# V of the second head group of batch 0 loaded ahead of all weights, into an output-weight buffer

## The chip, the cores and the metric

The kernel runs on 1 core of one Trainium2 chip. The metric is the device time of one execution in microseconds (us), less is better. Three executions of the kernel before took 917.45, 918.29 and 919.88 us; the median is 918.29 us.

## What is computed

An attention of Nystrom's kind feeds two gated feed-forward layers. B, H, S, D = 4, 8, 576, 64; 32 landmarks; 2304 tokens, model width 512, hidden width 1536.

```python
q_lm = q.reshape(B, H, m, S // m, D).mean(axis=3)      # m = 32
k_lm = k.reshape(B, H, m, S // m, D).mean(axis=3)
A  = sm(q, k_lm); Bm = sm(q_lm, k_lm); C = sm(q_lm, k) # softmax of the scaled product
Z = Bm^T / (norm1(Bm) * norminf(Bm) + 1e-06)           # norms of each matrix
for _ in range(6):
    Z = 2 * Z - Z @ Bm @ Z
attn = A @ Z @ C @ v
x  = silu(x @ w_gate) * (x @ w_val) @ w_out            # first layer, x from attn
x  = sigmoid(x @ w_gate2) * (x @ w_val2) @ w_out2      # second layer
```

All inputs and outputs are float32. V enters only in `C @ v`.

## The kernel before, in words

**Attention.** The eight heads of a batch are two groups of four, so there are eight pairs (b, g). For each pair a generator `front(b, g)` (F00, F01, F10, ... in the order string `first`, L575) does: K, then Q, summed over the 18 rows of a landmark on DVE (`lm`, L121), transposed on PE (`lt`, L125; `tp`, L135) and copied out by ACT; landmark scores (`cs`, L156), their exponentials on ACT (`e`, L162) and their transposes (`et`, L185, copied to `eT`, L186); then C @ V: 48 matmuls `cv` (L191) that read the tile `vin`, scaled on DVE into `bc` (L193); last the scores `as` (L204) with their maximum, difference and exponential (L207 to L210). `back(b)` (B0, B1, ...) takes the `bs` and `bc` of both groups of a batch: a chain of small DVE instructions makes the scale `rr` (L250 to L258), then come seven products `nw` (L267) on PE, each followed by one DVE instruction on `rw` (L273, L278 five times, L284), and a transpose to `ut` (L287). The products for group 1 read group 1's `bc`. While `back` iterates, it also steps `a_steps` (L213 to L228), the normalised and transposed A.

**First layer.** For chunk c of 256 hidden columns and batch b: `uw` (U00: `ut` times the input weights, L416), `gv1` (G00: gate and value matmuls into PSUM tiles `pg` and `pv`, Silu on ACT, product on DVE, split into a high and a low part) and `o1` (O00: `po`, added up in `acc`). The second layer, from about 250 us on, is not touched.

**Weights.** They arrive as pieces of 512 KB in three rotating `raw` buffers (L329). A piece of the input weights is four DMAs in layer 0 (L338), one of the output weights is one (L346). `convert` (L303) unpacks a piece with two ACT instructions (L314, L317) and two DVE instructions (L319, L323). For the output weights ACT and DVE then split the result (L350, L351) into the tile `wo` of tag "wo" (L368), of which there are two buffers of 8 KB a partition, one for each of two chunks in turn. Counted from 0, pieces 0 to 3 of chunk 0 are input weights, converted beside F00 (the word `I0`), and pieces 4 and 5 are its output weights; two pieces beyond the one in work are asked for ahead (`load_to`, L357).

**Loads of Q, K and V.** All are 576 KB DMAs on SP's queue, as are the weights, in one order. At the start K, Q, V of (0,0) and K, Q of (0,1) are issued (L294 to L296); there are four buffers for Q and K and one for V. Later ones are issued inside `front` by `load_next` (L85): K and Q two pairs ahead, as soon as their buffer is read; V one pair ahead, right after the `cv` matmuls that last read the single `vin` buffer (L194).

**The order of the work.** Python emits the instructions in the order of `first`, with weight conversions as filler between the words that begin with U, G or O. A scheduler at build time then gives each engine its final order, from the emitted order as a priority and from its own estimate of when operands are ready; each engine, and SP's queue, runs its list strictly in order. So an instruction can stand behind others that the code names later: in the trace the 54 last `as` matmuls of F01 stand ahead of its `cv`, though the code names `cv` first.

Of the kernel before, what the change touches and what calls it, by code (L numbers as in the profile page):

```python
# [5 lines left out]
F32 = mybir.dt.float32  # L6
# [8 lines left out]
def nystrom_moe_kernel(tc, q, k, v, wg1, wv1, wo1, wg2, wv2, wo2, out):  # L15
    nc = tc.nc
    B, H, S, D = q.shape
    M = 32
    P = 128
    L = S // M  # L20
    R = 6
    TP = S // R
    HS = S // 2
    DM = H * D
# [7 lines left out]
    def pool(name, side=None, **kw):  # L32
        return tc.alloc_tile_pool(name=name, bufs=1, side=side, reuse_waits="tile", **kw)

    cst = pool("cst")
    per = pool("per")
    att = pool("att")
# [28 lines left out]
    inq = {}  # L66

    def load_attn(b, which, g):
        if which == "v":
            t = att.tile([TP, 4, R, D], F32, tag="vin", name=f"vin{b}_{g}", bufs=1)  # L70
            nc.sync.dma_start(t, v[b, 4 * g:4 * g + 4].rearrange("h (p r) d -> p h r d", r=R))
        else:
            t = att.tile([P, L, D], F32, tag="in", name=f"{which}in{b}_{g}", bufs=4)
            src = {"q": q, "k": k}[which]
            nc.sync.dma_start(t, src[b, 4 * g:4 * g + 4].rearrange("h (t u) d -> (h t) u d", u=L))
        inq[which, b, g] = t
# [3 lines left out]
    AORDER = [(b, g) for b in range(B) for g in range(2)]  # L80
# [2 lines left out]
        return x.rearrange("p a b -> p (a b)")  # L83

    def load_next(b, g, which):  # L85
        i = AORDER.index((b, g)) + (1 if which == "v" else 2)
        if i < len(AORDER):
            load_attn(AORDER[i][0], which, AORDER[i][1])

    def step(fill, n=1):  # L90
# [20 lines left out]
    def front(b, g):  # L111
# [6 lines left out]
        def lm_steps(which):  # L118
            src = inq[which, b, g]
            lm = sm("lm", [P, 2, D])  # L120
            nc.vector.tensor_reduce(lm[:, 0], src.rearrange("p u d -> p d u"), axis=AX.X, op=ALU.add)  # L121
            nc.scalar.copy(lm[:, 1], lm[:, 0])
            yield
            ps = pst(b, [P, P], "lt", g)
            nc.tensor.transpose(ps, flat(lm), ident)  # L125
            bdt = sm("bd" + which, [P, 2, P], 1)
            for w in range(2):
                nc.scalar.activation(bdt[:, w], ps, AF.Copy, scale=pmask[:, w:w + 1])
            yield
            t = sm("kq", [P, NU, P])  # L130
            for i in range(3):
                ps = pst(b, [P, 3, P], "tp", g)
                for j in range(3):
                    u = 3 * i + j
                    nc.tensor.transpose(ps[:, j], flat(src[:, 2 * u:2 * u + 2]), ident)  # L135
                nc.scalar.copy(t[:, 3 * i:3 * i + 3], ps)
                yield
            load_next(b, g, which)
            return bdt, t
# [49 lines left out]
        for r in range(R):  # L189
            for h in range(4):  # L190
                mm(ps[32 * h:32 * h + 32, :], eT[:, r, 32 * h:32 * h + 32],  # L191
                   inq["v", b, g][:, h, r, :], start=(r == 0), stop=(r == R - 1))
        nc.vector.tensor_scalar(BC[:, g, M:M + D], ps, rc, None, op0=ALU.mult)  # L193
        load_next(b, g, "v")  # L194
        yield

# [95 lines left out]
            yield  # L292

    for g in range(2):  # L294
        for x in "kqv" if g == 0 else "kq":
            load_attn(0, x, g)  # L296


# [359 lines left out]
```

## Time and profile before

| | |
|---|---|
| runs | 917.45, 918.29, 919.88 us, median 918.29 |
| profiled execution, its own time | 917.74 us |
| span of its trace, first to last instruction | 915.9 us |
| PE busy / DVE busy / ACT busy | 877.8 / 542.2 / 391.7 us |
| granted TensorE clock, mean over the span | 0.987 of full speed |
| DMA moved | 57.66 MB |

The profiled execution lies 0.55 us under the median of the runs, and its trace leaves 1.84 us of its time outside the span. Times of rows are microseconds from the span's start unless they are marked ns. PE is TensorE, DVE VectorE, ACT ScalarE; SPq is SyncE's queue, which issues DMAs. A line such as L193 is a line of the kernel's code; matmuls issued through the helper `mm` all have line L62 and are told apart by their tiles. An instruction "waits" for what ended the idle time of its engine before it.

### The profile page before, as it was taken

How to read it: one execution, taken by the hardware profiler on the slowest of the kernel's cores; microseconds unless marked ns; L12 is line 12 of the kernel's file. 1: busy time of each engine (PE TensorE's matmuls, PEld its weight loads, DVE VectorE, ACT ScalarE, POOL GpSimd, SP SyncE). 2: the span in 40 equal slices, each digit the busy share in tenths (PEclk: the TensorE clock that was granted, in tenths of full speed). 3: DMA queues.
4: the chain of work that ended last, by engine and by line, in shares of the span. 5: the costliest groups of instructions: out<-in, count | busy, mean ns of one | idle time of the engine just before them, and what ended most of it. 6: DMA issues, size and time to landing. Idle time of an engine off the chain costs nothing.

```text
span 915.9 us, 16047 instructions
## 1 busy us (share of the span) xinstructions
PE 877.8 (96%) x6588; PEld 741.9 (81%) x6588; DVE 542.2 (59%) x1093; ACT 391.7 (43%) x853; POOL 0.7 (0%) x6
## 2 busy tenths in 40 slices
PE   5499899999999999999999999999999999999997
PEld 4356877778898998998998888888888888888886
DVE  6988857746968678769961154346238236323343
ACT  5568568545725446428652263134116114111111
POOL 0000000000000000000000000000000000000000
PEclk9599999999999999999999999999999999999999
DMA  7666211003513113203110022003004000000132
GB/s 230 222 209 182 70 53 49 7 1 93 155 31 93 47 47 116 69 1 95 46 44 4 0 71 68 1 28 110 0 1 138 1 1 24 1 0 1 47 93 69
DMA packets 27081, 57.66 MB, mean 63 GB/s; under 512 B 4224, under 2 KB 7296, under 8 KB 27008
## 3 DMA queue, kind: packets, MB, share of 16 engines
q1 hardware_dynamic: 25280, 54.28, 19.6%
q10 hardware_dynamic: 1728, 2.36, 1.1%
q8 instruction: 51, 0.84, 0.4%
q14 instruction: 22, 0.18, 0.1%
HBM read 51.90 MB, written 4.72 MB: 62 GB/s over the span
## 4 chain that ended last, share of the span: by engine, by line
PE 88%; DVE 5%; ACT 4%; DMA 1%; issue 1%; SPq 0%; ACTq 0%
PE po L62 33%; PE pg L62 24%; PE pv L62 23%; PE pu L62 3%; PE tp L135 2%; PE nw L62 1%; DMA qin<-in_q_dram 1%; DVE lm L121 1%; PE cs L62 1%; ACT e L162 1%; PE as L62 1%; DVE hl L351 0%; ACT L162 0%; PE et L185 0%; DVE h L441 0%
## 5 line engine op out<-in xcount | busy, mean ns | idle before, releaser
L62 PE MATMUL po<-hh,wo 128*128 128x288 f32 x768 | 162.1, 302 | 1.1 <-DVE uw L351 0.7
L512 DVE TENSOR_TENSOR hf<-hf,pv 128x512 f32<-128x512 f32 (+1 forms) x60 | 38.0, 634 | 193.0 <-PE pv L62 193.0
L62 PE MATMUL po<-wo,h 128*128 128x512 f32 x648 | 152.2, 390 | 0.0
L62 PEld LDWEIGHTS po<-wo,h 128*128 128x128 f32 x648 | 121.1, 188 | 25.4 <-ACT h L350 0.3
L62 PEld LDWEIGHTS po<-hh,wo 128*128 128x128 f32 x768 | 123.0, 188 | 21.1 <-issue 14.4
L62 PE MATMUL pg<-AH,w 128*128 128x512 f32 (+1 forms) x480 | 136.1, 368 | 0.0
L62 PE MATMUL pv<-AH,w 128*128 128x512 f32 (+1 forms) x480 | 136.0, 368 | 0.0
L62 PE MATMUL po<-hl,wo 128*128 128x288 f32 x384 | 114.8, 299 | 0.3 <-DVE hl L351 0.3
L511 ACT ACTIVATE hf<-pg 128x512 f32<-128x512 f32 (+1 forms) x60 | 33.2, 554 | 165.4 <-PE pg L62 158.3
L62 PE MATMUL pg<-AH,uw 128*128 128x288 f32 x576 | 98.7, 298 | 2.3 <-ACT uw L350 1.8
L62 PEld LDWEIGHTS pg<-AH,w 128*128 128x128 f32 x480 | 87.3, 188 | 15.4
L62 PEld LDWEIGHTS pv<-AH,w 128*128 128x128 f32 x480 | 87.1, 189 | 15.0
L62 PE MATMUL pv<-AH,uw 128*128 128x288 f32 x576 | 96.7, 296 | 1.2 <-ACT sg L439 1.2
L62 PEld LDWEIGHTS pg<-AH,uw 128*128 128x128 f32 x576 | 83.1, 188 | 8.4 <-ACT uw L350 4.9
L350 ACT CAST h<-hf 128x512 fp32r<-128x512 f32 (+1 forms) x60 | 34.6, 576 | 123.2 <-DVE hf L512 123.2
L533 DVE TENSOR_TENSOR oacc<-po,oacc 128x512 f32<-128x512 f32 x90 | 61.9, 691 | 41.1 <-PE po L62 39.9
L62 PEld LDWEIGHTS pv<-AH,uw 128*128 128x128 f32 x576 | 82.9, 188 | 3.2 <-ACT sg L439 2.2
L62 PE MATMUL pg<-x1l,w 128*128 128x512 f32 x192 | 74.7, 389 | 0.0
L62 PE MATMUL pv<-x1l,w 128*128 128x512 f32 x192 | 74.7, 389 | 0.0
L62 PEld LDWEIGHTS po<-hl,wo 128*128 128x128 f32 x384 | 72.3, 188 | 2.4 <-issue 0.9
L467 DVE TENSOR_TENSOR acc<-po,acc 128x288 f32<-128x288 f32 x128 | 56.0, 452 | 18.2 <-PE po L62 17.5
L439 ACT ACTIVATE sg<-pg 128x288 f32<-128x288 f32 x96 | 39.2, 409 | 51.7 <-PE pg L62 51.1
(113 smaller groups left out, 1062.8 us busy)
## 6 DMA issues: line engine op xcount, KB each, us to landing
raw<-in_moe_w_out_dram SPq DMA_DIRECT2D x24, 512.0 KB, 4.2
raw<-in_moe_w_gate_dram SPq DMA_DIRECT2D x48, 128.0 KB, 3.3
raw<-in_moe_w_val_dram SPq DMA_DIRECT2D x48, 128.0 KB, 3.1
raw<-in_moe_w_gate_dram SPq DMA_DIRECT2D x24, 256.0 KB, 2.9
raw<-in_moe_w_val_dram SPq DMA_DIRECT2D x24, 256.0 KB, 3.3
kin<-in_k_dram SPq DMA_DIRECT2D x8, 576.0 KB, 3.9
qin<-in_q_dram SPq DMA_DIRECT2D x8, 576.0 KB, 5.7
vin<-in_v_dram SPq DMA_DIRECT2D x8, 576.0 KB, 4.9
```

The costliest lines, as they stand in the source:

```text
L62: nc.tensor.matmul(o, l, r, start=start, stop=stop, skip_group_check=True)
L121: nc.vector.tensor_reduce(lm[:, 0], src.rearrange("p u d -> p d u"), axis=AX.X, op=ALU.add)
L135: nc.tensor.transpose(ps[:, j], flat(src[:, 2 * u:2 * u + 2]), ident)
L162: nc.scalar.activation(e[:, :, w].rearrange("p r t j -> p j r t"), pcs[w].rearrange("p (j r) t -> p j r t", r=3), AF.Exp, bias=nmx, scale= ...
L350: nc.scalar.copy(hi, x)
L439: nc.scalar.activation(sg, pss[0], AF.Silu)
L467: nc.vector.tensor_tensor(sl, ps, sl, op=ALU.add)
L511: nc.scalar.activation(h, pss[0], AF.Sigmoid)
L512: nc.vector.tensor_tensor(h, h, pss[1], op=ALU.mult)
L533: nc.vector.tensor_tensor(acc, ps, acc, op=ALU.add)
```

## The change

V of (0,1) is loaded with the first loads, behind Q of (0,1) and ahead of every weight, into a tile that is cut from a buffer of tag "wo" (96 of 128 partitions, 1536 of 2048 columns). The single `vin` buffer then serves the other seven, and `load_next` issues V of (1,0) where it issued V of (0,1), nothing at the end of `cv` of (0,1), and the rest as before. The output weights of chunk 1, the second user after it of the same buffer, must wait until `cv` of (0,1) has read it. No arithmetic changes.

```diff
     def load_attn(b, which, g):
         if which == "v":
-            t = att.tile([TP, 4, R, D], F32, tag="vin", name=f"vin{b}_{g}", bufs=1)
+            if (b, g) == (0, 1):
+
+                t = per.tile([P, 4 * DM], F32, tag="wo", name="vin0_1", bufs=2)
+                t = t[0:TP, 0:4 * R * D].rearrange("p (h r d) -> p h r d", h=4, r=R)
+            else:
+                t = att.tile([TP, 4, R, D], F32, tag="vin", name=f"vin{b}_{g}", bufs=1)
             nc.sync.dma_start(t, v[b, 4 * g:4 * g + 4].rearrange("h (p r) d -> p h r d", r=R))
...
     def load_next(b, g, which):
-        i = AORDER.index((b, g)) + (1 if which == "v" else 2)
-        if i < len(AORDER):
+        i = AORDER.index((b, g)) + 2
+        if which == "v" and i > 2:
+            i -= 1
+        if i < len(AORDER) and (which, *AORDER[i]) not in inq:
             load_attn(AORDER[i][0], which, AORDER[i][1])
...
     for g in range(2):
-        for x in "kqv" if g == 0 else "kq":
+        for x in "kqv":
             load_attn(0, x, g)
```

## Rows read from the trace of the kernel before

**Rows 1.** Busy time of each engine by stage, with granted clock (PEclk) and DMA.
```profile
0.00:16.00 16.00, 7.11 (x59) 5.62 (x59) 9.78 (x12) 6.68 (x19) 0.70 (x6) 1.00 0.92 270
16.00:28.60 12.60, 8.78 (x217) 6.38 (x219) 9.73 (x28) 12.10 (x34) 0.00 (x0) 0.83 0.72 234
28.60:42.84 14.24, 3.25 (x88) 2.23 (x80) 14.24 (x31) 6.77 (x15) 0.00 (x0) 0.50 0.73 216
42.84:60.79 17.95, 16.11 (x291) 9.12 (x292) 13.76 (x29) 9.26 (x26) 0.00 (x0) 0.85 0.51 150
60.79:110.00 49.21, 44.90 (x628) 34.52 (x628) 44.65 (x98) 40.40 (x98) 0.00 (x0) 1.00 0.53 160
110.00:140.00 30.00, 29.67 (x344) 22.92 (x342) 17.67 (x48) 15.75 (x37) 0.00 (x0) 1.00 0.20 57
```

**Rows 2.** Waits of PE from 28 to 60 us: total, times, longest.
```profile
PE nw L62 <- DVE bc L193: 5.4, 1, 5.4
PE cv L62 <- DMA vin<-in_v_dram: 3.5, 1, 3.5
PE nw L62 <- ACT bc L241: 2.1, 1, 2.1
```

**Rows 3.** Chain that ended last: start, us, what; a "..." skips DVE alone from 28.60 to 42.59.
```profile
28.60 0.49 DVE amx L207
...
42.59 0.20 DVE bc L193
...
108.69 6.49 PE po L62 x48
```

**Rows 4.** Instructions in order of time, SP's queue: the DMA issues around V of (0,1) and (1,0).
```profile
28.29 1.24 SPq L338 DMA_DIRECT2D raw<-in_moe_w_val_dram  x2
...
29.63 0.53 SPq L71 DMA_DIRECT2D vin<-in_v_dram  x1
...
37.08 0.33 SPq L71 DMA_DIRECT2D vin<-in_v_dram  x1
```

**Rows 5.** In order of time, ACT and PE: what `cv` of (0,1) needs, and itself.
```profile
27.78 0.48 ACT L186 COPY eT<-et 96x384 f32<-96x384 f32 x1 [0.16 <-PE et L185]
...
35.52 1.51 PE L62 MATMUL cv<-vin,eT 96*32 96x64 f32 x48 [3.46 <-DMA vin<-in_v_dram]
```

**Rows 6.** In order of time, DVE: from the scale `rr` to the first `rw`.
```profile
38.53 0.15 DVE L258 RECIPROCAL rr<-rr 128x2 f32<-128x2 f32 x1
...
38.67 0.68 DVE L323 SCALAR_TENSOR_TENSOR cv<-cv,cv 128x512 uint32<-128x512 uint32 x1
...
41.95 0.64 DVE L323 SCALAR_TENSOR_TENSOR cv<-cv,cv 128x512 uint32<-128x512 uint32 x1
...
43.45 0.36 DVE L273 TENSOR_TENSOR rw<-nw,rr 128x192 f32<-128x192 f32 x1
```

**Rows 7.** The fourth DMA of weight piece 0: its issue and its time to landing.
```profile
L338 SPq DMA_DIRECT2D raw<-in_moe_w_val_dram x1: 722/722/722, 5.1 to 5.1; - x1
...
DMA to landing us min/median/max: 9.0/9.0/9.0
```

**Rows 8.** In order of time, ACT: first and second weight conversion; PE: `cv` of (1,0); ACT: second chunk's `wo`.
```profile
16.41 0.68 ACT L314 ACTIVATE cv<-raw 128x512 f32<-128x512 f32 x1
...
19.49 0.70 ACT L314 ACTIVATE cv<-raw 128x512 f32<-128x512 f32 x1
...
55.82 0.38 PEld L62 LDWEIGHTS cv<-vin,eT 96*32 96x32 f32 x24 [0.46 <-ACT eT L186]
...
80.07 0.62 ACT L350 CAST wo<-cv 128x512 fp32r<-128x512 f32 x1
```

**Rows 9.** In order of time, PE: the first `pg`; ACT: the first load of the Silu table.
```profile
60.79 0.40 PE L62 MATMUL pg<-AH,uw 128*128 128x288 f32 x1 [0.41 <-ACT uw L350]
...
64.14 1.28 ACT L439 ACT_TABLE_LOAD   x1
65.43 0.41 ACT L439 ACTIVATE sg<-pg 128x288 f32<-128x288 f32 x1
```

## The prediction

> **What bounds the kernel now.** I read the busy times by stage first. From 60.79 us on PE sets the end: 44.90 of 49.21 us busy, then 29.67 of 30.00 [rows 1], and it stays so. Whatever is gained must therefore come from the first 61 us, and it reaches the end only if the PE work behind it moves up as a whole. There the stage from 28.60 to 42.84 us stands out: PE is busy 3.25 of 14.24 us, at a granted clock of 0.50 (the 1.2 GHz level), while DVE is busy for all 14.24 us [rows 1].
>
> The waits of PE say why it stands still: 2.1 us for ACT's `bc`, 3.5 us for V of (0,1) and 5.4 us for DVE's `bc` of group 1, 11.0 us together [rows 2]. The second is the load that the change moves. The eT that `cv` also needs is complete at 27.78 + 0.48 = 28.26 us, and `cv` starts at 35.52 [rows 5]. V was issued at 29.63, right behind the last DMAs of a weight piece at 28.29 [rows 4]; its landing is the end of the 3.5 us wait. But the longer wait comes after it: the last matmul of `cv` ends at 35.52 + 1.51 = 37.03 [rows 5], and the `bc` made of it runs on DVE at 42.59 [rows 3]. The chain of waits does not go through the load at all: it runs over DVE alone from 28.60 until `bc` [rows 3]. `bc` waits there for its turn. It stands behind unpacking of weights and behind steps of A, which the order made at build puts first because V was taken to be late. So the load costs time in two ways: by arriving late, and by having put `bc` at the back of DVE's list. The second is what the Newton products wait for.
>
> **The change part by part.**
>
> *The removed wait.* With V in SBUF, `cv` follows eT at 28.26; its 1.51 us give 29.8, and `bc` (0.27 us) can follow at about 30.1. Both first products can then run with ACT's copy of `bs`, which the 2.1 us wait ends on, shortly after 31 us. The first `rw` needs these and `rr`, and `rr` ends at 38.53 + 0.15 = 38.68 [rows 6]. `bc` now takes its 0.27 us of DVE ahead of `rr`, which makes 38.95; with a hand-over of 0.05 us, `rw` starts at 39.0 in place of 43.45, so **4.4 us** earlier. The bounds: nothing, if the new order still leaves `bc` or `rw` behind the weights; and at most the 11.0 us that PE waits in this stretch [rows 2], if the order also brings the chain to `rr` forward. I take 4.4, because nothing in the change touches what stands ahead of `rr`.
>
> *The work put back.* Behind `rr` and ahead of `bc`, from 38.67 to 41.95 + 0.64 = 42.59, DVE did seven instructions of other work in 3.92 us [rows 6]: unpacking of weight pieces 4 and 5, one split, steps of A. It is not gone. It now runs between the Newton steps or after them. DVE has 17.95 - 13.76 = 4.19 us idle up to 60.79 and 49.21 - 44.65 = 4.56 us up to 110, and then 12.33 us more [rows 1]. If all of that idle is usable it costs nothing; if DVE sets the pace until 110, all 3.92 us come back. I take 1.1 us, a good quarter, nearer to nothing because PE has other work to go on with: at 108.69 us it runs 48 output matmuls in 6.49 us without a break [rows 3] which were ready to be drawn forward, and DVE is only 59% busy after that [rows 1].
>
> The Trainium skill, Perfetto Trace Analysis, section Identifying the Most-Contended Engine, has it that the engine with the highest occupancy is the one to be relieved first. Taken by that, the stage belongs to DVE, whose work the change does not cut, the 3.92 us come back in full, and the sum would be a gain of some 0.5 us. I go by the gap on PE instead: DVE's list in this stage holds work that nothing needs soon.
>
> *V ahead of the weights.* 576 x 1024 bytes at the 270 GB/s of the first 16 us [rows 1] are 2.2 us by which the first three weight pieces land later. The last DMA of piece 0 lands at 5.1 + 9.0 = 14.1 us [rows 7], then at 16.3; ACT unpacks it at 16.41 [rows 8]. Piece 1, 512 KB or 1.9 us behind it, then lands at some 18.2 and is unpacked at 19.49 [rows 8]. So it is just hidden: cost nothing, at most 2.2 us if ACT's list puts the unpacking ahead (ACT is busy 12.10 of 12.60 us there [rows 1], so a stall would not be made good). Piece 3 waits for the `raw` buffer that ACT frees with piece 0, so from there on nothing is later.
>
> *SP's queue.* V of (1,0) goes where V of (0,1) was, at 29.63, instead of 37.08 [rows 4]. Its buffer is free by then, since `cv` of (0,0) is long done. It is needed at 55.82 [rows 8], some 20 us after landing: nothing. What stood behind it on SP at 37.08 next waits for K's buffer anyway. One DMA issue of 0.33 to 0.53 us is moved, none added.
>
> *The borrowed buffer.* The second chunk's output weights are first written at 80.07 [rows 8], some 50 us after `cv` has read V: nothing, also if `cv` came as late as before.
>
> *The clock.* PE ran at 0.50 until 42.84 and at a mean of 0.85 in the next stage [rows 1]. Work that starts 4.4 us earlier may raise the clock earlier too. That is worth between nothing and the slowed part of the next stage, (1.00 - 0.85) x 17.95 = 2.7 us; as PE still stands idle from the first products, shortly after 31, to 39.0, I take nothing.
>
> **Sum:** -4.4 + 1.1 = -3.3 us. Against the profiled execution's own 917.74 that is 914.4; the median of the runs lies 0.55 us above that execution, so **915.0** stands against 918.29, or -0.36%. About 0.3%, 2.75 us, is what a measurement of this kernel can tell from no change.
>
> **The rivals.**
>
> 1. *DVE takes it back.* The put-back work lands where DVE is 91% busy (44.65 of 49.21 us), and the dense stage starts earlier but goes slower. For it: DVE is full from 28.6 to 42.84 and nearly so to 110 [rows 1]. Against: PE's 6.49 us of unbroken output matmuls [rows 3]. Gain 4.4 - 3.9 = 0.5 us: 917.8, no change.
>
> The rule weighed above, of the Trainium skill's Perfetto Trace Analysis, comes to this rival.
>
> 2. *Slower: ACT changes its function tables more often.* The exponentials of (1,0) and (1,1) and the Silu of the first chunk share ACT from 60.79 to 110, where ACT is busy 40.40 of 49.21 us [rows 1]. If the first chunk comes 4.4 us sooner but F10 does not, the two alternate more. A table load is 1.28 us of ACT: it starts at 64.14, and the Silu behind it at 65.43 [rows 9]. An extra change there and back is 2.57 us. Two take 5.1 us and leave 918.3 - 3.3 + 5.1 = 920.1, still no change; from the third on, 7.7 us, it is 922.7, slower. For it: the order is made anew for everything up to some 200 us. Against: F10 is held up by the same PE list, behind the same `nw`, and should move along.
>
> The Trainium skill, ScalarE: Activation LUTs, section What ACT_TABLE_LOAD costs, adds a drain to each load, about 2.66 us in all. The rows show no drain behind the load; by the page two extra changes there and back would cost 10.6 us and be enough for slower.
>
> 3. *It does little of what it says.* The build's order might still take V as late, since it stands behind five loads of the same size, and keep `bc` where it is: 918.3. Against: six such loads are 3.54 MB, 13.1 us at 270 GB/s [rows 1], and eT is complete only at 28.26 [rows 5].
>
> 4. *More than forecast.* The chain to `rr` moves up as well, or the clock rises earlier: 6 to 8 us, 910.3 to 912.3. For it: DVE's B0 work ahead of `rr` is only a small part of the 10.1 us from 28.60 to 38.68. Against: what fills it is ready work, as before.
>
> **How the numbers follow.** Forecast 0.42, its own range 911.0 to 915.5 (gains of 7.3 to 2.8 us); rival 4 0.10; rival 1 0.24; rival 3 0.08; rival 2, with its third change, 0.16. Faster is 0.42 + 0.10 = 0.52, the same 0.24 + 0.08 = 0.32, slower 0.16. The predicted time is the forecast's, 915.0. The range takes in rivals 1 and 3, the stall of 2.2 us at the first unpacking on top of them (918.3 + 2.2 = 920.5) and the larger half of rival 4: 910.5 to 920.5.
>
> **What would show it.** Right: V's issue among the first six on SP, `cv` of (0,1) behind eT before 31 us, `bc` on DVE at 29 to 32, PE's 3.5 and 5.4 us waits gone, `rw` at about 39, the first `pg` at about 56 to 57 in place of 60.79 [rows 9], and a stage to 110 with no more PE idle than its 49.21 - 44.90 = 4.3 us now. Piece 0 should land at 16 and no ACT wait for `raw` should appear before 28 us. Wrong: `bc` still behind weights (rival 3); `pg` early but more PE idle than 4.3 us by 110, with DVE as what it waits for (rival 1), or with more table loads on ACT before 110 than now (rival 2). A gain that comes from anywhere behind 140 us would make the working wrong even if the time is right.

## The result, and the profile after

The changed kernel takes **929.25 us** (median of 4 runs, 923.96 to 930.17) against 918.23 us (917.45 to 919.88): 1.0106 times the time before, 95% interval 1.0065 to 1.0146. It is slower by some 11 us, where 3.3 us less were forecast. The profiled execution took 929.54 us, with a span of 927.8 us (before: 915.9). PE was busy for 891.2 us of it (before: 877.8) and idle for 36.6 (38.1): PE does the same 6,588 matmuls, waits a little less, and takes 13.4 us longer over them.

Busy time by stage, columns as in [rows 1]:

```profile
28.60:42.84 14.24, 9.39 (x167) 7.06 (x167) 12.23 (x25) 9.40 (x22) 0.00 (x0) 0.62 0.77 254
42.84:60.79 17.95, 14.85 (x246) 7.93 (x243) 14.57 (x29) 7.75 (x20) 0.00 (x0) 0.76 0.41 117
60.79:110.00 49.21, 43.70 (x557) 28.29 (x557) 36.68 (x85) 35.10 (x82) 0.00 (x0) 0.86 0.50 144
```

The stage that was to gain has gained: PE is busy for 9.39 us from 28.60 to 42.84, before 3.25. The loss is in the third line. In the same 49.21 us PE finishes 557 matmuls instead of 628, it is nearly as busy as before, and the mean granted clock is 0.86 instead of 1.00. DVE and ACT are less busy than before, not more.

The instructions that answer to [rows 5, 6, 9], in order of time on ACT, PE and DVE:

```profile
28.61 0.47 ACT L193 COPY eT<-et 96x384 f32<-96x384 f32 x1 [0.17 <-PE et L192]
28.73 0.32 PE L62 MATMUL cv<-vin,eT 96*32 96x64 f32 x2
30.49 0.28 DVE L200 TENSOR_SCALAR bc<-cv,rc 128x64 f32<-128x64 f32 x1 [0.77 <-PE cv L62]
38.87 0.35 DVE L280 TENSOR_TENSOR rw<-nw,rr 128x192 f32<-128x192 f32 x1
59.78 0.40 PE L62 MATMUL pg<-AH,uw 128*128 128x288 f32 x1 [0.69 <-ACT uw L357]
```

`cv` follows eT, `bc` is made at 30.49 instead of 42.59, and the first `rw` starts at 38.87 instead of 43.45: 4.6 us earlier. Of this 1.0 us is left at the first `pg` (59.78 against 60.79). Then it turns. SP's queue, which answers to [rows 4], and its longest wait from 40 to 60 us (total, times, longest):

```profile
33.51 0.53 SPq L76 DMA_DIRECT2D vin<-in_v_dram  x1
...
45.41 1.24 SPq L345 DMA_DIRECT2D raw<-in_moe_w_val_dram  x2
55.87 0.33 SPq L76 DMA_DIRECT2D vin<-in_v_dram  x1
56.30 1.10 SPq L345 DMA_DIRECT2D raw<-in_moe_w_gate_dram  x2
```

```profile
SPq L76 <- PE cv L62: 9.1, 1, 9.1
```

V of (1,0) goes at 33.51. Its successor V of (1,1) shares one buffer with it and has to wait on SP until `cv` of (1,0) has read it: 9.1 us, to 55.87. Behind it stands the ninth weight piece (the third input piece of the second chunk), which therefore starts at 56.30. In the kernel before it was ahead of that load, which waited 2.0 us there:

```profile
51.78 1.18 SPq L338 DMA_DIRECT2D raw<-in_moe_w_gate_dram  x2
...
57.87 0.33 SPq L71 DMA_DIRECT2D vin<-in_v_dram  x1
```

DVE unpacks the second chunk's last two input pieces at 73.01 and 84.80. Before, the last one came at 72.20. In order of time, on DVE:

```profile
73.01 0.67 DVE L330 SCALAR_TENSOR_TENSOR w<-cv,cv 128x512 uint32<-128x512 uint32 x1
84.80 0.67 DVE L330 SCALAR_TENSOR_TENSOR w<-cv,cv 128x512 uint32<-128x512 uint32 x1
```

```profile
72.20 0.70 DVE L323 SCALAR_TENSOR_TENSOR w<-cv,cv 128x512 uint32<-128x512 uint32 x1
```

The last piece is not this late because its data are. Its last load is issued at 67.28 and lands 4.4 us later, at 71.7. ACT comes to it only at 79.53, having waited for no DMA from 60 us on. In order of time, SP's queue and ACT of the changed kernel:

```profile
67.28 0.47 SPq L345 DMA_DIRECT2D raw<-in_moe_w_val_dram  x1
...
79.53 0.69 ACT L321 ACTIVATE cv<-raw 128x512 f32<-128x512 f32 x1
```

So some 8 us of the delay on ACT are the place that the order made at build gives the unpacking. The build made that order with V(1,1) ahead of the weights; how late it took them to be is not on record.

The second chunk's `pu` needs that piece and, at tag `o` of PSUM (two buffers), holds both buffers until its result is copied out. The output products `po` use the same tag, and stand behind `pu` on PE's list as well; which of the two holds them is not separated. `po`, which began at 81.15 before, begins at 96.19, on PE of the changed kernel:

```profile
85.75 1.91 PE L62 MATMUL pu<-w,ut 64*32 64x512 f32 x2
...
88.00 1.91 PE L62 MATMUL pu<-w,ut 64*32 64x512 f32 x2
...
96.19 0.53 PE L62 MATMUL po<-hh,wo 128*128 128x288 f32 x2
```

From about 75 us on PE thus lacks the large products that stood between the small steps before. How its clock goes meanwhile shows in the busy times of chosen stretches (columns as in [rows 1]; the seventh number is the granted clock). Before, there was one half-clock stretch:

```profile
24.40:48.30 23.90, 12.03 (x189) 8.52 (x190) 22.30 (x46) 13.81 (x34) 0.00 (x0) 0.50 0.64 197
```

After, there are five. The other lines are what stood ahead of some of them:

```profile
24.40:31.30 6.90, 5.19 (x126) 4.34 (x126) 6.06 (x23) 5.51 (x13) 0.00 (x0) 0.51 0.84 300
31.30:34.70 3.40, 0.55 (x22) 0.32 (x16) 3.40 (x6) 1.20 (x3) 0.00 (x0) 0.98 0.49 147
34.70:44.90 10.20, 8.20 (x58) 4.88 (x62) 8.59 (x18) 6.94 (x18) 0.00 (x0) 0.51 0.73 240
51.70:58.60 6.90, 6.90 (x139) 3.81 (x138) 5.51 (x11) 1.40 (x4) 0.00 (x0) 0.51 0.22 67
75.00:79.00 4.00, 1.24 (x24) 0.77 (x28) 1.93 (x10) 3.96 (x7) 0.00 (x0) 0.99 0.00 0
79.00:82.50 3.50, 3.50 (x132) 3.25 (x120) 3.33 (x12) 2.93 (x7) 0.00 (x0) 0.52 0.28 67
82.50:85.90 3.40, 2.11 (x19) 1.22 (x12) 3.35 (x10) 3.00 (x8) 0.00 (x0) 0.98 1.06 254
85.90:96.10 10.20, 10.20 (x72) 4.10 (x71) 4.33 (x10) 4.59 (x11) 0.00 (x0) 0.51 0.28 88
```

Before, the clock was at its lower level (1.2 GHz) for 23.9 us, of which PE worked 12.0. Now it is there for 37.7 us in all and PE works through 34.0 of them (5.19 + 8.20 + 6.90 + 3.50 + 10.20). An **account** follows, used below for other kernels too: span = idle time of PE + its busy time, and of the busy time half of what lies at half clock is put down to the clock. That half is an estimate: it takes work there to be twice as long as at 2.4 GHz, as the first two `pu` are (1.91 against 1.04 us). For small products it is too much: the 16 matmuls of a Newton product take 0.86 against 0.53 us. If it is fair, what remains should be about the same in every kernel.

| kernel (profiled run) | span | PE idle | PE busy | of it at half clock | busy less half of that |
|---|---|---|---|---|---|
| before | 915.9 | 38.1 | 877.8 | 12.0 | 871.8 |
| after | 927.8 | 36.6 | 891.2 | 34.0 | 874.2 |

By the account the 11.9 us are -1.5 of idle time, +11.0 of clock and +2.4 of a rest that is not explained. How far it can be trusted is shown behind experiment 8.

### The profile page after: what moved, and what is told of

It is laid out like the page before. It is cut to its first block, busy times and chain, and to the rows that moved or that the text cites. A ratio compares the mean times of both kernels' runs of the same rounds, so it can differ in the third digit from the quotient of the medians.

```text
span 927.8 us, 16049 instructions
## 1 busy us (share of the span) xinstructions
PE 891.2 (96%) x6588; PEld 747.4 (81%) x6588; DVE 542.4 (58%) x1093; ACT 392.8 (42%) x853; POOL 0.7 (0%) x6
## 4 chain that ended last, share of the span: by engine, by line
PE 89%; DVE 5%; ACT 3%; issue 1%; DMA 1%; SPq 0%; ACTq 0%; DVEq 0%
PE po L62 33%; PE pg L62 23%; PE pv L62 23%; PE pu L62 4%; DVE lm L128 1%; PE nw L62 1%; PE tp L142 1%; PE as L62 1%; PE cs L62 1%; DMA kin<-in_k_dram 1%; PE cv L62 1%; DVE cv L326 1%; PE et L192 0%; DVE hl L358 0%; DVE uw L358 0%
## 5 line engine op out<-in xcount | busy, mean ns | idle before, releaser
L62 PEld LDWEIGHTS po<-hh,wo 128*128 128x128 f32 x768 | 122.8, 188 | 20.5 <-issue 13.0
L540 DVE TENSOR_TENSOR oacc<-po,oacc 128x512 f32<-128x512 f32 x90 | 61.8, 691 | 40.7 <-PE po L62 39.5
```

The costliest lines, as they stand in the source:

```text
L62: nc.tensor.matmul(o, l, r, start=start, stop=stop, skip_group_check=True)
L540: nc.vector.tensor_tensor(acc, ps, acc, op=ALU.add)
```

## The experiments

Three theories. **Queue**: V(1,1), put ahead of the weights on SP, costs the time. **Clock**: PE works where its clock is at half. **Order**: the order made anew at build costs, apart from both. The forecast's rivals on DVE and ACT are judged from the trace in the next section.

**1. The changed kernel again**, no edit.

> The changed kernel once more, for the spread of its time. Its four runs so far fall into 929 to 930 us at a mean granted TensorE clock of 0.978 to 0.979 and one of 924.0 at 0.988, which is about the clock of the kernel before (0.987), with the same instructions in the same order. Theory 'clock' (PE stands on small tiles alone for stretches and runs them at 1.2 GHz): time and mean clock go together again, some 5 us for 0.009 of clock, and a part of about 6 us over the kernel before stays also at 0.988. Theory 'order alone' (the order of work costs all 11 us): runs at different clocks take the same time.

Measured: 928.59 us (925.15 to 929.16, 6 runs) against 918.01 (17 runs), 1.0108 (1.009 to 1.0125). The loss stands. The single runs add something: of the changed kernel's ten runs in both sets, eight have a mean clock of 0.978 to 0.981 and 928.0 to 930.2 us, one has 0.985 and 925.15, one 0.988 and 923.96. The same instructions in the same order take 4 to 5 us less in these two, which go with a higher mean clock. The kernel before has 916.7 to 918.5 us at 0.988, so by that one run some 6 us are lost at an equal mean clock too.

**2. All V of batches 1 to 3 issued from POOL instead of SP**, in the changed kernel and, as a control, in the kernel before (there V(0,1) as well).

```diff
-            nc.sync.dma_start(t, v[b, ...
+            (nc.gpsimd if b else nc.sync).dma_start(t, v[b, ...
```

> The changed kernel, with V of batches 1 to 3 loaded from POOL's queue in place of SP's; V of batch 0 stays in front on SP. Theory 'queue' (V of (1,1) stands on SP ahead of the input weights of chunk 1 and waits 9.1 us for cv of (1,0); the fourth of these weight pieces is then unpacked at 84.8 us instead of 72.2, the half-done pu holds both PSUM buffers of its tag, and po starts at 96 instead of 81): pieces 8 and 9 are issued before 55 us, the last w of chunk 1 is unpacked near 72, po starts near 80, the clock stays full from 60 us on, and the time falls to 918 or below, 914 to 915 if the forecast's gain comes through. Theory 'clock' alone: the clock still falls between 79 and 96 and the time stays at 925 to 930. Theory 'order anew' (any other order is as bad): anything, with po not near 80.

> Control: the kernel before, with V of all pairs but the first loaded from POOL's queue. V of (0,1) still waits for the vin buffer but no longer stands behind the weights on SP. Theory 'queue': SP's waits for V in the kernel before are short (its V of (1,1) stands behind pieces 7 and 8), so it changes little, 915 to 920; V of (0,1) lands some 7 us earlier, so up to 4 us faster is possible. If it gains as much over before as e2 gains over the changed kernel (over 8 us), the queue was a cost of both kernels and not of the change.

Measured: 922.68 us, 1.0052 (1.0034 to 1.0069); the control 918.74, 0.9998 (0.9986 to 1.0009). About half of the loss goes when these loads leave SP's queue, and POOL as issuer is no gain by itself.

**3. The late piece first**: in `uw_steps` the heads in the order 3, 2, 1, 0, so that `pu` takes its buffers only when the last piece is there.

```diff
-            for h in range(4):
+            for h in (3, 2, 1, 0):
```

> The changed kernel, with the four head terms of pu (U words) computed in the order 3, 2, 1, 0, so that the first matmul of a pu needs the last weight piece and the pu can't hold PSUM half done. Loads and waits on SP are as emitted in the changed kernel. Theory 'queue', with PSUM as its link: the late weights stay late (last w of chunk 1 near 85) but po or the B1 products no longer wait behind the half-done pu; the time falls by 3 to 8 us, to 921 to 926. If PSUM is no link: 928 to 930. Theory 'clock' alone: the clock still falls in 79 to 96 and the time stays.

Measured: 925.45 us, 1.0077 (1.0057 to 1.0096). The Newton products of batch 1 come earlier (1.3 us early to 5.7 late against the kernel before; in the changed kernel 2.0 to 8.2 late), but `po` still begins at 98.11, and the piece is as late as before (unpacked at 86.72). The clock is at half for longer than in any other kernel here, five stretches with 42.4 us of PE's work; from 50.9 to 64.6 and from 85.1 to 98.7 are the longest. So under a third of the loss goes with a mere change of order, and most stays.

**4. One load alone.** V(1,1) from POOL, everything else in the code of the changed kernel as it is. The order made at build follows: it is the old one up to 68.7 us on ACT, 71.2 on PE and 75.1 on DVE, and another from there on.

```diff
+            (nc.gpsimd if (b, g) == (1, 1) else nc.sync).dma_start(t, v[b, ...
```

> The changed kernel with one load alone, V of batch 1's second head group, issued from POOL; V of (1,0) stays in front of K and Q on SP, and the batches 2 and 3 stay on SP. Theory 'queue': of the 10.6 us lost, about 6 came back when V of batches 1 to 3 all went by POOL; if it is this one load that held SP for 9.1 us (waiting for its buffer, with weights p8 and p9 behind it), the same comes back here: 921.5 to 923.5. Theory 'several loads': other V loads wait ahead of weights too, and this one gives at most half of it: 925 to 927. Theory 'order anew': the build's new order of B1's steps is what costs, not the wait: 926 to 929. In the trace: with 'queue' the second chunk's first weights are unpacked before 62 and PE's half-clock stretch at 86 to 96 is gone.

Measured: **922.68 us**, 1.0044 (1.0027 to 1.006): this one load gives back at least what all V loads together gave: 0.64%, or 5.9 us. SP's queue there, and the last input piece on ACT:

```profile
46.34 1.18 SPq L345 DMA_DIRECT2D raw<-in_moe_w_gate_dram  x2
47.56 1.23 SPq L345 DMA_DIRECT2D raw<-in_moe_w_val_dram  x2
48.90 1.87 SPq L345 DMA_DIRECT2D raw<-in_moe_w_gate_dram  x2
50.81 0.60 SPq L345 DMA_DIRECT2D raw<-in_moe_w_val_dram  x1
64.18 0.33 SPq L80 DMA_DIRECT2D kin<-in_k_dram  x1
64.56 0.47 SPq L345 DMA_DIRECT2D raw<-in_moe_w_val_dram  x1
...
69.75 0.71 ACT L321 ACTIVATE cv<-raw 128x512 f32<-128x512 f32 x1
```

The ninth piece goes at 46.34 instead of 56.30. That alone does not bring its unpacking forward (74.06 on DVE, 73.01 in the changed kernel). The last input piece gains: ACT's list now has it at 69.75, right behind the ninth, and DVE finishes it from 76.25 on. `po` begins at 86.47, and there is no half-clock stretch behind 63.5 us. The first unpacking of the chunk stayed at 62.85, where before 62 was expected; in the kernel before it comes at 51.23. So what V(1,1) costs on SP is shown, 5.9 us; how much of it is its wait and how much the order that the build makes with it there, this run does not separate. The lines show a second load of the same sort: K(2,1) waits 12.9 us for its buffer and holds the last quarter of the last input piece.

The Trainium skill, DMA: Bandwidth & Descriptors, section Issuing engines are not separate DMA queues, says that issuing from several engines saves only the sequencer's time for the issue. Here that is 0.33 us, and 5.9 us came back. What was saved is not the issue but a wait of 9.1 us for a buffer at the head of SP's queue, with the order that went with it.

**5. The rest of SP's queue.** K(2,1) from POOL as well; then K, Q and V of batches 2 and 3 too, so that SP has weights alone from the seventh piece on; and the latter in the kernel before. In the two changed kernels the order on PE, DVE and ACT is that of experiment 4 throughout.

```diff
+            (nc.gpsimd if (which, b, g) == ("k", 2, 1) else nc.sync).dma_start(t, src[b, ...
```

> The kernel with V(1,1) on POOL (922.7), and K(2,1) on POOL too; PE's order is the same. In its trace K(2,1) stands on SP ahead of the last load of the second chunk's last input piece and waits 12.9 us for its buffer (51 to 64 us), so that this piece is unpacked at 76.3 (72.2 in the kernel before). Theory 'queue': what is left of the loss is this second head-of-line wait: the piece is unpacked by 68, the second chunk's products and po start 3 to 5 us earlier, and the time is 917.5 to 920.5. Rival 'clock and order': the 4.5 us left are work that fell into half-clock stretches before 64 us, which this load doesn't touch: 922 to 923.5.

> V(1,1) and all K, Q and V of batches 2 and 3 on POOL: from the seventh weight piece on SP has weights alone; PE's order is again the same. Theory 'queue': no load waits ahead of a weight any more: at or below the one before, 914 to 920. Rival 'clock and order': 922 to 923.5. Rival 'POOL starts loads late': over 923.5, with waits of PE for K or Q of batch 2 in the waits.

> The kernel before with V(1,1) and all K, Q and V of batches 2 and 3 on POOL, the control. Theory 'queue': there the second chunk's pieces had no such wait in front of them, so little changes: 916 to 919; if the one before is below this by over 1 us, V in front of the weights is worth something once its queue is clear.

Measured: 921.81 us, 1.0038 (1.0024 to 1.0053); 922.43, 1.0044 (1.003 to 1.0059); the kernel before 917.92, 0.9994 (0.9984 to 1.0004). The queue theory said 917.5 to 920.5 for the first and fails here: all of the piece now lands early, but DVE unpacks it at 74.85 against 76.25, because ACT and DVE come to it when their own order says so. With the order as it is, the 4 us that are left are not SP's waits.

**6. The wait put into the kernel before.** A copy of one column from batch 1's `bc` into the ninth piece's raw tile, overwritten by its load, makes this load wait as it does behind V(1,1).

```diff
         t = raw_tile()
+        if (layer, c, kk) == (0, 1, 2):
+            nc.vector.tensor_copy(t[:, :, 0], BS[1][2][:, 0, M:M + 2].bitcast(U32))
```

> The converse: the kernel before, in which a copy of one column from batch 1's bc into the ninth piece's raw tile (overwritten by its load at once) makes this piece's load wait until V's product of (1,0) is done, as it does behind V(1,1) in the changed kernel; V of (0,1) is where it was. The piece then goes at about 58 to 59 instead of 51.8. Theory 'queue': the wait alone makes the kernel before slower, by 3 to 7 us: 921 to 925. Rival 'order and clock of the early start': the wait is cheap without the early V: 917 to 920.

Measured: 921.9 us (919.89 to 925.46), 1.0038 (1.0023 to 1.0053). V(0,1) is where it was, and the held load costs 3 us. That is not the wait alone: the order made at build is another from 58 us on ACT and 61 us on PE. Its SP queue and two stretches:

```profile
57.63 0.33 SPq L71 DMA_DIRECT2D vin<-in_v_dram  x1
59.29 1.10 SPq L340 DMA_DIRECT2D raw<-in_moe_w_gate_dram  x2
```

```profile
24.40:48.30 23.90, 12.34 (x191) 8.82 (x191) 22.32 (x46) 13.57 (x34) 0.00 (x0) 0.50 0.70 198
79.00:89.20 10.20, 8.73 (x98) 5.12 (x97) 7.17 (x20) 7.21 (x18) 0.00 (x0) 0.50 0.49 129
```

The piece goes 7.5 us later (59.29 against 51.78), `po` begins at 91.02 instead of 81.15, and in the profiled run (923.45 us) a half-clock stretch appears at 79.0 to 89.2 that the kernel before does not have. By the account below it is 4.6 of the 5.0 us by which this run's span is longer. But the single runs do not bear out that the clock is the way: the one with the highest mean clock, 0.989, took 922.45 us, above the median.

**7. Filler matmuls.** `warm` issues `n` f32 matmuls of the identity with an operand that is just in use, into a PSUM buffer nobody reads. First three behind each Newton product of batch 0 and four behind each of its two small score products (in the changed kernel and the kernel before), and in one kernel one behind each product of batch 1.

```diff
+    def warm(nm, b, x):
+        n = WARM.get((nm, b), 0)
+        if n:
+            ps = ptile([P, x.shape[-1]], "gv", f"wm_{nm}_{b}")
+            for _ in range(n):
+                mm(ps, ident, x)
```

> The changed kernel with filler matmuls on PE whose results nobody reads: three of 128x192 behind each of the seven Newton products of batch 0, and four of 128x256 behind each of batch 0's two 32x32 score products; nothing else changes, though the order built from it may shift a little. Theory 'clock': half-clock stretches follow stretches with little matmul work, so with the gaps of 30 to 52 us filled the stretches 34.7 to 44.9 and 51.7 to 58.6 shrink or go. PE was busy for 8.2 and 6.8 us in them, so up to 7.5 us come back; the fillers cost PE some 10 us, of it in gaps nearly all (PE idles 12 us of 28 to 52): 922 to 927. Theory 'queue alone': the clock is not what the time hangs on, PE waits for weights later anyway: 928 to 930. Theory 'fillers in the way': they delay the Newton steps, and the time is 930 to 934.

> As the one before, and one filler matmul of 128x192 behind each of the seven Newton products of batch 1 too. Theory 'clock': the half-clock stretch at 85.9 to 96.1, in which PE was busy for 10.2 us, follows the idle stretch at 75 to 87, and seven fillers of some 0.3 us each may hold it off: up to 5 us less than without them, 918 to 923. Theory 'queue alone': PE waits there for the second chunk's weights whatever its clock, and the fillers only add: the same as the one before or up to 2 us more.

> The kernel before with the same filler matmuls in batch 0 as the first of the two. Theory 'clock': PE was busy for 12.0 of the 23.9 us of half clock at 24.4 to 48.3, so up to 6.0 us can come back where that work lies on the path: 912 to 917. Theory 'hidden there': at half clock PE still idled for 11.8 us, so its speed was not what the stretch hung on, DVE (busy 22.3 of 23.9) was: 917 to 919. 'Fillers in the way': over 920.

Measured: 921.95 us, 1.0039 (1.0024 to 1.0054); 936.01, 1.0193; the kernel before with fillers 921.62, 1.0036. None of the three settles anything. The fillers changed the order made at build. In the first V(1,1) fell back behind the ninth piece, which undoes the wait as experiment 4 does. In the second the first `pg` came at 92.12, with PE busy until then; the fillers share PSUM buffers with the dense products, but that this is the reason is not shown. In the third the fillers took 13.7 us of PE, and the half-clock work fell only from 12.0 to 6.4 us.

**8. Ten fillers where the order stays.** Behind batch 0's first Newton product alone, into the gap before 35 us; the order of everything else on PE, DVE, ACT and SP is then unchanged throughout. In the changed kernel, and in that of experiment 4; in a last one also a single filler behind each later product of batch 0, which does shift the order.

```diff
-    WARM = {}
+    WARM = {("nw0", 0): 10}
```

> The changed kernel with ten filler matmuls of 128x192 behind batch 0's first Newton product, into a PSUM buffer nobody reads, where PE idles for 3.6 us (31.9 to 35.4); the order of the other instructions on PE and of all loads on SP stays as it is. Theory 'clock': the half-clock stretch 34.7 to 44.9 follows this gap; with it filled the stretch begins later or is shorter, and the work in it (PE busy for 8.2 us) comes up to 4 us earlier, but V(1,1) still waits on SP for the product behind that work and the second chunk's weights behind V(1,1): they come earlier by as much, and the time falls by 1 to 5 us, to 924 to 927.5. Rival 'clock hidden': DVE's chain sets the Newton steps and what follows, the clock there costs nothing: 928 to 929.5. Rival 'fillers in the way': over 930.

> The same ten fillers in the kernel that issues V(1,1) alone from POOL (922.7), its order on PE and SP unchanged too. Theory 'clock': what is left of the loss there, 4.5 us, is half-clock time that now falls on work (PE busy 21.9 us at half clock against 12.1 in the kernel before, 4.9 us lost): with the stretch 36.1 to 46.4 (9.0 us busy) shortened, 1 to 4 us come back: 918.5 to 921.7. Rival 'order anew': what is left is the new order of the later steps: 922 to 923.5.

> As the one before, and one filler behind each of batch 0's six later Newton products, which does shift the build's order. Theory 'clock': the gaps of 47 to 52 us, which come ahead of the half-clock stretch at 53 to 63 (9.6 us busy), are filled too: 916 to 919, so level with the kernel before or faster. Rival 'order anew': the order decides, 920 to 925.

Measured: 926.98 us (925.58 to 931.0), 1.0092 (1.0059 to 1.0124); 922.24, 1.0028 (1.0013 to 1.0043); 925.25, 1.0064 (1.0039 to 1.0088). By the times the first two are not apart from the same kernels without fillers, 1.0108 and 1.0044; the second median lies in the range of the rival, not in that of the clock theory, and the third kernel is outright slower than that of experiment 4. The trace of the first shows what the clock did. Its own lines come first; the third fence has the fourth Newton product of batch 0, with the fillers and, below it, in the changed kernel:

```profile
31.83 3.52 PE L62 MATMUL wm_nw<-bc,ident 128*128 128x192 f32 x20
```

```profile
31.60:48.70 17.10, 12.40 (x179) 8.26 (x167) 16.73 (x32) 10.22 (x25) 0.00 (x0) 1.00 0.73 235
```

```profile
42.68 0.53 PE L62 MATMUL nw<-rw 32*32 32x96 f32 x16
44.83 0.53 PE L62 MATMUL nw<-rw 32*32 32x96 f32 x16
```

With the gap filled the stretch at 34.7 to 44.9 is gone, the granted clock is 1.00 from 31.6 to 48.7, and the span is 2.0 us shorter. The order is the same in both, so the gain can be followed: the second Newton product comes 0.1 us earlier (39.16 against 39.28), the fourth 2.1, and 2.0 are left at the end. In the kernel of experiment 4 the fillers shorten the stretch from 36.1 to 46.4 to one from 40.7 to 44.1. So in these traces the gap brought on the half clock, and the half clock cost time: half of the 4.1 us that the account gives for the stretch's 8.20 us of work. Part of the rest went into waits, as the rival said: the second Newton product waits 1.51 us for DVE's `rw`, without fillers 0.90.

The account of the profiled runs, with the lines that concern the cause:

| kernel | span | PE idle | PE busy | of it at half clock | busy less half of that |
|---|---|---|---|---|---|
| heads reversed (experiment 3) | 923.6 | 34.5 | 889.1 | 42.4 | 867.9 |
| V(1,1) on POOL | 921.2 | 36.5 | 884.7 | 21.9 | 873.7 |
| V(1,1) and K(2,1) on POOL | 919.8 | 35.7 | 884.1 | 20.5 | 873.9 |
| before, ninth piece held | 920.9 | 38.0 | 882.9 | 21.1 | 872.3 |
| after, ten fillers (3.5 us of PE) | 925.8 | 34.3 | 891.5 | 25.7 | 878.6 |

The last column lies between 3.9 us under and 3.3 over 871.8 (the 3.5 us of fillers taken off), and the changed kernel's second profile (experiment 1) has 875.7, 3.9 over: the account is good to some 4 us, no better. The first line speaks against it: with 8.4 us more of half-clock work than the changed kernel, experiment 3 is 4.2 us shorter. Of the 3.9 us that "V(1,1) and K(2,1) on POOL" has above the kernel before, -2.4 are idle time, +4.2 clock and +2.1 the rest. That is within what the account can miss. So the cause of the 4 us that are left stays open between the clock and the new order of the work; no run isolates either.

## Why the prediction was wrong

*The removed wait: right.* 4.4 us were forecast at the first `rw`, and it came 4.6 earlier, by the steps given: `cv` behind eT, `bc` at 30.49, `rw` behind `rr`. But the first `pg`, forecast at 56 to 57, came at 59.78. The last Newton product was still 4.9 us early (48.70 against 53.56); the rest of it was lost up to the first `pg`, with PE at half clock and without a gap from 51.7 to 58.6.

*The work put back: no harm.* DVE is idle for 49.21 - 36.68 = 12.5 us of the stage to 110. Rival 1 did not come true: DVE and ACT are less busy in that stage than before. The Trainium skill, Perfetto Trace Analysis, section Identifying the Most-Contended Engine, would have the engine with the highest occupancy optimized first. What the prediction worked out by that rule, all 3.92 us of DVE's work back, did not come about.

*V ahead of the weights: harmless, but not as worked out.* The last DMA of piece 0 lands at 17.0 instead of 14.1, 2.9 us later, where 2.2 were forecast. ACT's first conversion starts at 18.63 instead of 16.41 [rows 8]. That this is the upper bound of 2.2 us is luck: ACT waits for no DMA there, its list has exponentials and copies first. It did not hold up `rw`.

*SP's queue: **the step that failed**.* "It is needed at 55.82, some 20 us after landing: nothing. What stood behind it on SP at 37.08 next waits for K's buffer anyway." The step followed V(1,0) and stopped there. The next load into the same buffer, V(1,1), moved too: the order made at build put it ahead of the ninth weight piece, where it waited 9.1 us. Why the build did so is not on record. In its place on SP, with the order that the build makes for it, this one load cost 5.9 of the 10 to 11 us (experiment 4), and a like wait without the early V costs 3 us (experiment 6). The prediction had named the place of this danger (a queue's loads and their waits) and looked at one load of it.

*The clock: a bound with the wrong sign left out.* "Between nothing and" a gain of 2.7 us was the range. By the account, good to some 4 us, the clock took 11.0 us, part of it behind the late weights. Before, PE idled through 11.9 of the 23.9 us at half clock, most of it in the stage from 28.60 to 42.84 [rows 1]; for that time the account charges nothing. After, the removed wait brings work into it. New half-clock stretches follow gaps at 31 to 35 and 75 to 79 us, and PE is busy for most or all of them; that the gap brings the stretch was tried for the first alone (experiment 8). The Trainium skill, TensorE: Matmul & The Clock Gate, section HAM oscillation — how this bites in real kernels, puts the cost of such stretches at half their length. By that rule of the Trainium skill an estimate is (37.7 - 23.9) / 2 = 6.9 us; the account says more, because before half of the length was idle.

*The borrowed buffer: right.* The second chunk's `wo` is first written at 102.27, long after `cv`.

*The rivals.* Rival 2 had the sign and, at 922.7, a price on the right side, but not the cause: there are 14 table loads up to 200 us before and after. The mark set for the stage to 110, no more than 4.3 us of idle PE, was missed by 1.2 (49.21 - 43.70 = 5.5), and PE's longest wait in it is 2.5 us for ACT's copy of eT, with fewer table loads than before up to 110 us (5 against 6).

## What to carry to other kernels

When a load is moved, follow every later load into the same buffer, too: ask where each now stands in its queue, what it waits for there, and what stands behind it. Then look at when the data land and when the engine comes to them: here the last piece lay ready for 8 us, because the order made at build had changed with the load. And count a wait of PE by the clock it falls into: time in which PE idles at half clock hides what the clock costs, work that is moved into it is slowed, and a gap can slow the work behind it (filling one of 3.6 us gave 2.0 us back).

## What the runs showed that was not expected

A full PE does not mean a full clock. From 85.9 to 96.1 us PE was busy for 10.20 of 10.20 us at 0.51, and from 51.7 to 58.6 for 6.90 of 6.90; the gaps stood ahead of these stretches (4.39 us busy of 6.80 from 44.9 to 51.7, 2.11 of 3.40 from 82.5 to 85.9).

Gains and losses of the first 60 us were evened out later. In the control of experiment 2 the first dense product came 4.3 us earlier than in the kernel before, and from 180 us on everything ran at the same time as there. No version tried beats the kernel before by more than can be measured (best: 0.9994).
